# A Fourier layer with top-k experts on one core: first-stage groups placed in pairs, tables in twelve tiles, another expert gate and another key search

## The chip, the core and the metric

The kernel runs on one core of a Trainium2 chip. The metric is the device time of one execution in microseconds (us); lower is better. The engines that matter are TensorE (PE, with its weight loads shown apart as PEld), VectorE (DVE), ScalarE (ACT), GpSimd (POOL) and the queue of SyncE (SP), from which nearly all DMAs are issued.

## The reference, cut to what matters

Two layers follow each other on x of shape 8 x 3136 x 256. First a spectral layer: a real FFT over the 3136 positions, a complex 256 x 256 linear map with bias, a soft threshold on real and imaginary parts, and the inverse FFT. Then, in each of the 8 batches, a score per position, the 128 highest positions, an expert (256 -> 1024 -> 256, ReLU) on those rows only, weighted by a sigmoid of the score and added.

```python
X = np.fft.rfft(x, axis=1)                       # x: 8 x 3136 x 256
Yr = Xr @ w_r - Xi @ w_i + b_r
Yi = Xr @ w_i + Xi @ w_r + b_i
Yr = np.sign(Yr) * np.maximum(np.abs(Yr) - 0.01, 0.0)   # Yi likewise
y = np.fft.irfft(Y, n=3136, axis=1)
scores = y @ w_gate                              # 8 x 3136
for b in range(8):
    top = np.argpartition(-scores[b], 128)[:128]
    xe = y[b, top]
    ye = np.maximum(xe @ w1, 0) @ w2
    out[b, top] = xe + ye / (1 + np.exp(-scores[b, top]))[:, None]
```

## The kernel before

The FFT of length 3136 = 98 x 32 is done in two stages of small matmuls. **First stage** (`s1`): eight groups per batch; GpSimd or VectorE makes the sum and the difference of two halves of x (`xu`, `xv`, in `xsum_side`), TensorE multiplies them by a table (`quarters`: quadrants of 64 x 64 of the array, into two `s` banks of PSUM), ScalarE copies the banks out, and the result goes to scratch memory in HBM (`As`). **Second stage** (`s2`): per batch six units (`Q = 6`, so `T = 48` units in all); a unit loads 16 rows of `As` (tile `av`), does 64 small matmuls into the two `px` banks, and is split by ScalarE and VectorE into a high and a low part (`Xh`, `Xl`). **Spectral map** (`spectral`, full 128 x 128 array): 24 matmuls of 512 columns per unit into `py` banks, then bias and threshold (`shrink`). **Inverse** (`s2i`, 32 matmuls on strips of 32 rows into four `s` banks; then `s1i`, again eight groups per batch, with `cu`, `cv` and `cin` in the roles of `xu`, `xv` and `xt`) back to HBM through `Cs` and to the output. `s2i` also takes the score of each row of its banks (`score_part`).

**Selection** (`select`): the 128 highest scores of two batches together are found by a search over the bits of the threshold, three bits per round for the last two batches. A round counts by a bf16 comparison and a reduction on VectorE (`counts`), adds over the partitions by one small matmul (`ones`), and reads the counts (`digest`): which digits pass (`ok`), how many (`d`), the new prefix (`wp`, and a copy `w2`), and the keys of the next round (`f`), one after the other on VectorE. **Experts** (`gather`, `prepare`, `hidden`, `combine`): an indirect DMA fetches 128 rows, TensorE turns them, 32 plus 24 matmuls follow, and another indirect DMA scatters them into the output. The gate is a product and row sum on VectorE (`junk <- xe, wgb`) with a sigmoid on ScalarE. Experts use the two `py` banks.

The order of all instructions is fixed when the program is built: a planner keeps a clock per engine, and at every step picks among the candidates `middle` (spectral), `forward` (`s2`), `backward` (`s2i`), `forward1` (`s1`), `backward1` (`s1i`) and the threads of selection and experts the one with the least cost: the expected wait plus `STEP` times how far its place lies ahead of the current unit. The places of `s1` and `s1i` come from the lists `F1` and `I1` (units of a batch). Loads of constants wait for a number of stored and loaded pieces of batch 0 (`behind_a`, list `CA`). `warm` puts matmuls without use into gaps.

Of the kernel before, what the change touches and what calls it, by code (L numbers as in the profile page):

```python
# [22 lines left out]
P0 = 15  # L23
# [138 lines left out]
def fourier_moe(ctx: ExitStack, tc: tile.TileContext, x, w_r, w_i, b_r, b_i, wg, w1, w2,  # L162
# [184 lines left out]
    class Side:  # L347
        def __init__(self, g, low=None):
            self.g, self.over, self.need, self.low = g, False, None, low
            self.step()  # L350
# [14 lines left out]
    def side(g, low=None):  # L365
        s = Side(g, low)
        if not s.over:
            sides.append(s)
        return s
# [6 lines left out]
    def pump(t):  # L376
        again = True
        while again:
            again = False
            for s in list(sides):  # L380
                while not s.over:
                    w = s.when()
                    if w is None or w > t - (s.low() if s.low else 0.0):
                        break
                    s.step()
                    again = True
                    if s.low:
                        break
# [15 lines left out]

    first = c_tile([128, 2, 2, 64], F32, "first")
    sec = [c_tile([128, NJ, 64], F32, f"second{z}") for z in range(2)]
# [8 lines left out]
    wgb = c_tile([128, D], F32, "wgb")  # L415
    w1s = c_tile([128, 2, FF], F32, "w1s")
# [26 lines left out]
    def consts_s():  # L443
        yield "SP", behind_a(CA[0])
        ld(sec[0].rearrange("p j s -> p (j s)"), t_second[:, :NJ * 64])
        yield "SP", behind_a(CA[3])
        ld(tail, t_tail)
        yield "SP", behind_a(CA[4])
        ld(wgb, wg.rearrange("(o e) -> o e", o=1).broadcast_to([128, D]))
        ld(sec[1].rearrange("p j s -> p (j s)"), t_second[:, NJ * 64:])  # L450
# [16 lines left out]
    def consts_bias():  # L467
        vec.memset(m2l, -2.0 * LAM)
        yield "SP", behind_a(CA[2])
        for c, src in enumerate((b_r, b_i)):  # L470
            row = src.rearrange("(o e) -> o e", o=1)
            ld(bias[:, c, :], row.broadcast_to([128, D]))
            ld(bias_t[33 * c:33 + 31 * c], row.broadcast_to([33 - 2 * c, D]))
        yield "DVE", [bias, bias_t]
        vec.tensor_scalar(out=bias, in0=bias, scalar1=LAM, scalar2=None, op0=ALU.add)
        vec.tensor_scalar(out=bias_t, in0=bias_t, scalar1=LAM, scalar2=None, op0=ALU.add)
        made.add("bias")

    def consts_moe():
        yield "SP", lambda: pe["end"] if spec["t"] >= 1 else None  # L480
# [35 lines left out]
    def select(bs, bits, lag):  # L516
# [8 lines left out]
        low = lag  # L525

# [17 lines left out]
        def digest(tot, m, i, nxt):  # L544
# [31 lines left out]
            yield from counts(f, m2)  # L576

        rounds = [(2 ** (hi - i) - 1, i) for hi, i in zip([32] + cuts, cuts)]
        side(first_keys(rounds[0][0]), low)
        for (m, i), nxt in zip(rounds, rounds[1:] + [None]):  # L580
# [5 lines left out]
            hold(tot, name, side(digest(tot, m, i, nxt), low))  # L586
# [63 lines left out]
    def e_name():  # L650
        return "py" if spec["t"] >= T else m_name()

    def e_tile(shape):
        return new(ps, shape, F32, "py", 2) if spec["t"] >= T else m_tile(shape)

    def prepare(b, k, idx, xe, spare, st):
        n = min(128, cap - 128 * k)
        name = e_name()
        px = e_tile([128, 2, n])
# [4 lines left out]
        sg = new(pool, [n, 1], F32, "sg")  # L664
# [684 lines left out]
```

## Time and profile before

| what | us |
|---|---|
| median of 3 runs (700.66 to 705.55) | 703.77 |
| the profiled execution | 699.05 |
| its span, first to last instruction | 696.9 |
| TensorE busy | 672.4 (96%) |
| VectorE, ScalarE, GpSimd busy | 403.9, 360.1, 392.9 |
| DMA | 162.55 MB, mean 233 GB/s |

A busy time is a sum over instructions; matmuls overlap one another and their ends are modelled, so TensorE at 96% is not at its peak. The span falls into a start until the first spectral matmul, the spectral stage, and an end in which the last two batches are selected and all eight experts run.

### The profile page before, as it was taken

The numbers are of one execution on the slowest core, as the hardware profiler recorded it, in microseconds if no ns is written. First come the engines' busy times: TensorE is split into PE (matmuls) and PEld (weight loads), VectorE is DVE, ScalarE is ACT, GpSimd is POOL, SyncE is SP. The second block draws the span as 40 slices with busy tenths as digits, with TensorE's granted clock in tenths as the row PEclk, the third lists the DMA queues.
The fourth block names the chain that finished last, engine by engine and source line by source line (L and its number), as shares of the span: only waits on it lengthen the run. The fifth ranks groups of instructions, "written<-read, shape, count | busy, mean of one in ns | idle before, by whom it ended". The sixth has DMA issues, their size and how long they took to land.

```text
span 696.9 us, 19479 instructions
## 1 busy us (share of the span) xinstructions
PE 672.4 (96%) x7733; PEld 433.6 (62%) x7733; DVE 403.9 (58%) x1231; ACT 360.1 (52%) x766; POOL 392.9 (56%) x325
## 2 busy tenths in 40 slices
PE   8989999999999999999999999999999899989996
PEld 5546666566565656665566556666656566537896
DVE  7324454455356666774566676745776664478732
ACT  2335664655655656655566656565645445433111
POOL 4266654865866567767765767576434424453221
PEclk9989999999999999999999999999999999989999
DMA  8899878999799989998889889988794955584000
GB/s 237 283 288 304 264 241 260 252 302 270 224 234 302 285 292 200 319 276 287 197 326 274 311 212 327 273 265 187 257 265 131 213 156 161 175 246 147 31 31 24
DMA packets 85109, 162.55 MB, mean 233 GB/s; under 512 B 6333, under 2 KB 58906, under 8 KB 85018
## 3 DMA queue, kind: packets, MB, share of 16 engines
q1 hardware_dynamic: 83962, 159.13, 77.1%
q0 software_dynamic: 1056, 2.17, 1.0%
q8 instruction: 61, 1.00, 0.6%
q14 instruction: 30, 0.25, 0.1%
HBM read 83.23 MB, written 78.12 MB: 232 GB/s over the span
## 4 chain that ended last, share of the span: by engine, by line
PE 78%; DMA 7%; DVE 6%; issue 5%; ACT 1%; POOL 1%; SPq 0%; POOLq 0%; DVEq 0%; ACTq 0%
PE py L272 43%; PE s L272 26%; PE px L272 9%; DMA cin<-Ct 1%; DMA cin<-Cs 1%; DMA xe<-in_moe_w 1%; DVE px L220 1%; DVE r L220 1%; DMA As<-ot 1%; DMA xt<-in_x 1%; DVE c L220 1%; DMA av<-As 1%; DMA As<-at 1%; DVE junk L220 1%; POOL out L723 0%
## 5 line engine op out<-in xcount | busy, mean ns | idle before, releaser
L272 PE MATMUL py<-wh,Xh 128*128 128x512 f32 x384 | 168.0, 438 | 0.1
L272 PE MATMUL py<-wl,Xh 128*128 128x512 f32 x384 | 150.8, 393 | 0.1
L272 PE MATMUL py<-wh,Xl 128*128 128x512 f32 x384 | 150.3, 391 | 0.0
L272 PEld LDWEIGHTS py<-wh,Xh 128*128 128x128 f32 x384 | 72.1, 188 | 84.7 <-issue 62.7
L220 POOL TENSOR_TENSOR xu<-xt 113x512 f32<-113x512 f32 x56 | 72.0, 1286 | 90.5 <-PE s L272 76.1
L220 POOL TENSOR_TENSOR cu<-cin 113x512 f32<-113x512 f32 x56 | 72.2, 1289 | 82.4 <-PE s L272 72.3
L220 DVE TENSOR_TENSOR Xl<-px,Xh 128x512 fp32r<-128x512 f32 x96 | 61.9, 686 | 86.0 <-ACT Xh L220 85.9
L220 DVE CUSTOM_DVE_ANT_0 junk<-s,wgb 128x256 f32<-128x256 f32 x192 | 81.0, 422 | 51.3 <-ACT ct L220 37.8
L220 ACT COPY ot<-s 113x512 f32<-113x512 f32 x136 | 72.7, 596 | 62.6 <-PE s L272 56.2
L220 POOL TENSOR_TENSOR cv<-cin 113x512 f32<-113x512 f32 x64 | 85.7, 1341 | 11.3 <-DMA cin<-Cs 6.6
L220 ACT COPY at<-s 113x512 f32<-113x512 f32 x120 | 64.5, 593 | 52.9 <-PE s L272 45.2
L220 POOL TENSOR_TENSOR Y<-r,r 128x512 f32<-128x512 f32 x48 | 61.8, 1287 | 49.8 <-ACT r L220 36.4
L220 POOL TENSOR_TENSOR xv<-xt 113x512 f32<-113x512 f32 x60 | 78.2, 1304 | 8.7 <-DVE xt L220 4.9
L272 PEld LDWEIGHTS py<-wl,Xh 128*128 128x128 f32 x384 | 72.1, 188 | 17.1 <-issue 0.5
L272 PE MATMUL s<-cu,first 49*64 49x512 f32 (+1 forms) x256 | 76.5, 621 | 2.2 <-DVE ok L220 1.5
L272 PEld LDWEIGHTS py<-wh,Xl 128*128 128x128 f32 x384 | 72.6, 189 | 9.2
L220 ACT COPY ct<-s 128x256 f32<-128x256 f32 x192 | 57.8, 388 | 31.5 <-PE s L272 31.0
L272 PE MATMUL s<-xu,first 64*64 64x512 f32 (+1 forms) x256 | 71.4, 620 | 1.6 <-POOL xu L220 1.6
L272 PE MATMUL s<-cv,first 49*64 49x512 f32 (+1 forms) x256 | 71.8, 624 | 0.0
L272 PEld LDWEIGHTS px<-second,av 64*64 64x64 f32 x3072 | 52.6, 136 | 30.5 <-issue 15.0
L272 PE MATMUL s<-xv,first 64*64 64x512 f32 (+1 forms) x256 | 70.0, 623 | 0.0
L220 ACT CAST Xh<-px 128x512 fp32r<-128x512 f32 x96 | 51.7, 593 | 34.2 <-PE px L272 33.9
(135 smaller groups left out, 1002.8 us busy)
## 6 DMA issues: line engine op xcount, KB each, us to landing
out<-ot SPq DMA_DIRECT2D x64, 392.0 KB
av<-As SPq DMA_DIRECT2D x48, 512.0 KB
Cs<-ct SPq DMA_DIRECT2D x48, 512.0 KB
cin<-Cs SPq DMA_DIRECT2D x64, 384.0 KB
xt<-in_x SPq DMA_DIRECT2D x60, 392.0 KB
As<-at SPq DMA_DIRECT2D x60, 392.0 KB
cin<-in_x SPq DMA_DIRECT2D x4, 392.0 KB
As<-ot SPq DMA_DIRECT2D x4, 392.0 KB
```

Source lines behind the costliest of these rows:

```text
L220: return f(*args, **kw)
L272: return nc.tensor.matmul(out, a, b, start=start, stop=stop)
```

## The change

All places are laid anew: `F1` and `I1` put the eight groups of each batch 0.75 units apart, and the `s1` of one batch and the `s1i` of another get the same place (a pair, `NQ = 2`); batch 1, for which there is no inverse yet, has places of its own (`FB`), and the second unit waits for the first four spectral steps (`K0`). The tables of the second stage lie in twelve tiles (`fwd`, `bwd`), of which only the first is loaded at the start; weights, biases, the other tables, w1 and w2 are loaded later. Sums of batch 0 go to VectorE, those of the last batch to GpSimd; clearing of buffers goes to GpSimd but for one. The experts' gate is two matmuls with one column on TensorE, and the turned rows are copied out by ScalarE; experts may use `s` banks once the inverse second stage is done. For the last two batches the next round's keys are made from the prefix before last (`g`), ahead of `wp` and `w2`, and other sides step back for that search (`prio`). The units of the last two steps shrink on VectorE. Several weights of the planner change.

```diff
+                    if s.prio == 2 and s.need[0] == "DVE":
+                        u = [x for x in (x.when() for x in sides if x.prio == 0) if x is not None]
+                        if u and min(u) < w + UR:
+                            break
...
-    sec = [c_tile([128, NJ, 64], F32, f"second{z}") for z in range(2)]
+    fwd, bwd = [[c_tile([128, 4, 64], F32, f"{n}{g}") for g in range(Q)] for n in ("fwd", "bwd")]
...
-        yield "SP", behind_a(CA[0])
-        ld(sec[0].rearrange("p j s -> p (j s)"), t_second[:, :NJ * 64])
...
+        for n, t, src, w in sorted([(CS[0][g], fwd[g], t_second, 4 * g) for g in range(Q)] + [(CS[1][g], bwd[g], t_second, NJ + 4 * g) for g in range(Q)]
+                                   + [(CA[3], tail, t_tail, None), (CA[4], wgb, wg, None)], key=lambda x: x[0]):
+            yield "SP", behind_a(n)
...
-        yield "SP", lambda: pe["end"] if spec["t"] >= 2 else None
+        yield "SP", lambda: pe["end"] if spec["t"] >= CM else None
         ld(w1s, w1.rearrange("(h p) f -> p h f", p=128))
+        ld(wgc, wg.rearrange("(h p o) -> p h o", p=128, o=1))
...
-            yield "SP", lambda: pe["end"] if spec["t"] >= 3 + k // 2 else None
+            yield "SP", lambda: pe["end"] if spec["t"] >= CM + 1 + k // CN else None
...
+                if fast and nxt:
+
+                    m2 = nxt[0]
+                    f = f[:, :, :m2]
+                    vec.scalar_tensor_tensor(out=f, in0=d.broadcast_to([N1, nb, m2]), scalar=i, in1=st["g"],
+                                             op0=ALU.logical_shift_left, op1=ALU.bitwise_xor)
+                    yield "DVE", []
+                    yield from counts(f, m2)
                 for o in (wp, w2) if i else (wp,):
                     vec.scalar_tensor_tensor(out=o, in0=d, scalar=i, in1=st["w"], op0=ALU.logical_shift_left, op1=ALU.bitwise_xor)
+                if fast and nxt:
+                    st["w"] = w2
+                    ahead_keys(wp, after)
+                    return
...
+        def ahead_keys(wp, after):
+            if after:
+                m3, i3 = after
+                st["g"] = new(pool, [N1, nb, m3], U32, "g" + tag, 1)
+                vec.tensor_tensor(out=st["g"], in0=digits[:, 8 * i3:8 * i3 + m3].rearrange("p (o m) -> p o m", o=1).broadcast_to([N1, nb, m3]),
+                                  in1=wp.broadcast_to([N1, nb, m3]), op=ALU.bitwise_xor)
...
     def e_name():
-        return "py" if spec["t"] >= T else m_name()
+        if spec["t"] < T:
+            return m_name()
+        return "s" if ES and s2m["t"] >= T and open_at("s") < open_at("py") else "py"
...
-            yield "DVE", [px]
-            vec.tensor_copy(xT, px)
+            yield "ACT", [px]
+            act.copy(out=xT, in_=px)
             st["xT"] = True
-            yield "DVE", [xe]
-            junk = new(pool, [n, D], F32, "junk", 1)
-            vec.tensor_tensor_reduce(out=junk, in0=xe, in1=wgb[:n], scale=1.0, scalar=0.0,
-                                     op0=ALU.mult, op1=ALU.add, accum_out=sg)
...
+        for h in range(2):
+            mm(sg, xT[:, h, :], wgc[:, h, :], h == 0, h == 1)
...
-                    adder(t, b == 0).tensor_tensor(out=o, in0=t[:, 0, :], in1=t[:, 1, :], op=op)
+                    adder(t, 2 * (b == 0)).tensor_tensor(out=o, in0=t[:, 0, :], in1=t[:, 1, :], op=op)
...
-                    adder(t, last).tensor_tensor(out=o, in0=t[:, 0, :], in1=t[:, 1, :], op=op)
+                    adder(t, LA if last else 0).tensor_tensor(out=o, in0=t[:, 0, :], in1=t[:, 1, :], op=op)
...
-    EARLY, AHEAD, SW = 0.6,1.1,0.2
+    EARLY, AHEAD, SW = 0.6,1.5,0.2
...
-    STEP, THW, FIL = 5,4,(4,3)
+    STEP, THW, FIL = 3,4,(8,0.5)
...
-    F1, I1 = [-1, 0, 0, 1, 2, 2, 3, 3],[10, 10, 11, 12, 12, 13, 14, 15]
+    F1, I1 = [-1.75, -1.0, -0.25, 0.5, 1.25, 2.0, 2.75, 3.5],[10.25, 11.0, 11.75, 12.5, 13.25, 14.0, 14.75, 15.5]
...
-    NQ = 1
-    CA = 1,2,8,9,10,9
+    NQ = 2
+    CA = 1, 8, 8, 12, 11, 0, 12
+    CS, CM = ((0, 8, 9, 10, 11, 12), (11, 12, 13, 14, 14, 14)),42
+    FB = .25, .5, .75, 1.25, 1.5, 2, 2.5, 3
+    CN, K0 = 4,4
+    WS = 1.0
+    CX = 10, 10, 10, 10, 11, 11, 11, 12
...
+    TE, LV, UR, FS, ES, LA, HP = 0,2,0.5,True,True,3,False
...
-        if n >= T or quad(n) not in av or n > spec["t"] + 1 or len(X) > 1:
+        if n >= T or quad(n) not in av or n > spec["t"] + 1 or len(X) > 1 or n == 1 and spec["k"] < K0:
...
-            vec.memset(t[:P0].rearrange("p a c -> p (a c)") if len(t.shape) == 3 else t[:P0].rearrange("p a c d -> p (a c d)"), 0.0)
+            (gps if z else vec).memset(t[:P0].rearrange("p a c -> p (a c)") if len(t.shape) == 3 else t[:P0].rearrange("p a c d -> p (a c d)"), 0.0)
...
-            if spec["t"] >= T or at == 0:
+            if spec["t"] >= T or at == 0 and (0, 7) in summed:
                 warm(c[1])
```

## Rows read from the trace of the kernel before

**Rows 1.** Windows: us, busy us per engine, clock, DMA share, GB/s

```profile
0.00:24.00 24.00, 20.68 (x103) 10.75 (x104) 16.96 (x19) 9.87 (x18) 13.26 (x12) 1.00 0.86 272
24.00:30.70 6.70, 6.70 (x31) 5.49 (x30) 0.30 (x1) 1.92 (x4) 0.00 (x0) 1.00 0.70 239
...
38.70:45.50 6.80, 6.79 (x29) 2.54 (x32) 0.00 (x0) 1.07 (x2) 5.34 (x5) 0.50 1.00 302
46.50:590.00 543.50, 534.99 (x6731) 338.09 (x6727) 324.96 (x1031) 314.93 (x674) 336.26 (x279) 1.00 0.87 255
590.00:635.00 45.00, 42.31 (x281) 21.62 (x280) 27.86 (x78) 19.91 (x42) 24.13 (x17) 0.89 0.69 199
635.00:692.00 57.00, 54.16 (x437) 50.23 (x429) 31.33 (x100) 10.48 (x26) 10.13 (x11) 1.00 0.12 40
```

**Rows 2.** Timeline of the start: start us, us, engine line op out<-in xcount

```profile
35.18 1.16 PE L272 MATMUL px<-second,av 64*64 64x64 f32 x64 [0.74 <-DMA av<-As]
...
37.00 1.29 DVE L220 TENSOR_TENSOR Xl<-px,Xh 128x512 fp32r<-128x512 f32 x2 [3.48 <-ACT Xh L220]
...
46.46 0.50 PE L272 MATMUL py<-wh,Xh 128*128 128x512 f32 x1
```

**Rows 3.** Chain that ended last, in order of time: start us, us, what

```profile
24.89 5.76 DMA As<-ot
...
43.59 1.92 PE s L272 x8
...
50.16 1.02 PE s L272 x8
...
571.02 1.58 PE py L272 x6
...
574.47 2.26 PE py L272 x9
...
582.63 1.73 PE s L272 x32
...
644.17 3.03 PE py L272 x24
```

**Rows 4.** Groups by line: busy us, mean ns of one, idle before

```profile
L220 ACT COPY ot<-s 113x512 f32<-113x512 f32 x136 | 72.7, 596 | 62.6 <-PE s L272 56.2 <-DMA out<-ot 4.1 <-PE px L272 1.2
...
L220 POOL TENSOR_TENSOR cu<-cin 113x512 f32<-113x512 f32 x56 | 72.2, 1289 | 82.4 <-PE s L272 72.3 <-DMA av<-As 5.2 <-DMA cin<-Ct 4.6
...
L220 DVE TENSOR_TENSOR cu<-cin 113x512 f32<-113x512 f32 x8 | 8.1, 1017 | 6.1 <-DMA cin<-Cs 3.4 <-PE s L272 1.6 <-DMA cin<-Ct 1.1
...
L220 DVE CUSTOM_DVE_ANT_0 junk<-xe,wgb 128x256 f32<-128x256 f32 x8 | 4.5, 558 | 0.0
...
L220 DVE SCALAR_TENSOR_TENSOR hl<-py,hh 128x512 fp32r<-128x512 f32 x10 | 6.9, 689 | 7.3 <-ACT hh L220 7.3
```

**Rows 5.** Timeline of VectorE in the last search

```profile
606.67 0.17 DVE L220 TENSOR_SCALAR px<-px 98x2 int32<-98x2 f32 x1 [3.42 <-PE px L272]
...
641.66 0.16 DVE L220 TENSOR_SCALAR ok<-px 98x14 f32<-98x14 f32 x1
...
642.06 0.17 DVE L220 SCALAR_TENSOR_TENSOR px<-px,w 98x2 uint32<-98x2 uint32 x1
642.26 0.16 DVE L220 SCALAR_TENSOR_TENSOR w<-px,w 98x2 uint32<-98x2 uint32 x1
...
644.53 0.16 DVE L220 TENSOR_SCALAR ok<-px 98x14 f32<-98x14 f32 x1
...
654.20 0.16 DVE L220 TENSOR_SCALAR px<-px 98x2 uint32<-98x2 f32 x1
...
663.25 0.16 DVE L220 TENSOR_TENSOR idxs<-col,px 128x2 uint32<-128x2 f32 x1
```

**Rows 6.** Timeline of TensorE in the expert after the search

```profile
664.38 3.74 PE L272 MATMUL py<-xT,w1s 128*128 128x128 f32 x32
```

**Rows 7.** Timeline of GpSimd: the last scatter

```profile
692.89 0.97 POOL L723 DMA_INDIRECT out<-ye,idxs  x1 [6.48 <-DVE ye L220]
```

More of the change, by code (lines that the diff above doesn't have):

```diff
@@ L347, in fourier_moe, with __init__ @@
     class Side:
-        def __init__(self, g, low=None):
-            self.g, self.over, self.need, self.low = g, False, None, low
+        def __init__(self, g, low=None, prio=1):
+            self.g, self.over, self.need, self.low, self.prio = g, False, None, low, prio
             self.step()
@@ L468, in consts_bias @@
         vec.memset(m2l, -2.0 * LAM)
[L469 to L477, printed above, removed]
+        for z, (t, n) in enumerate(((bias, 128), (bias_t, 33))):
+            yield "SP", behind_a(CA[2 + 4 * z])
+            for c, src in enumerate((b_r, b_i)):
+                row = src.rearrange("(o e) -> o e", o=1)
+                if z:
+                    ld(t[33 * c:33 + 31 * c], row.broadcast_to([33 - 2 * c, D]))
+                else:
+                    ld(t[:, c, :], row.broadcast_to([n, D]))
+            yield "DVE", [t]
+            vec.tensor_scalar(out=t, in0=t, scalar1=LAM, scalar2=None, op0=ALU.add)
+            made.add("bias" if z == 0 else "bias_t")
     def consts_moe():
-        yield "SP", lambda: pe["end"] if spec["t"] >= 1 else None
+        yield "SP", lambda: pe["end"] if spec["t"] >= 3 else None
         ld(wq, t_wq)
@@ L525, in select @@
         low = lag
+        last = bs.stop == B
+        fast = last and FS
         def counts(f, m):
@@ L576, in digest @@
             yield from counts(f, m2)
+            if fast:
+                ahead_keys(wp, after)
+        def ahead_keys(wp, after):
[4 more added lines that the diff above has]
+                                  in1=wp.broadcast_to([N1, nb, m3]), op=ALU.bitwise_xor)
         rounds = [(2 ** (hi - i) - 1, i) for hi, i in zip([32] + cuts, cuts)]
-        side(first_keys(rounds[0][0]), low)
-        for (m, i), nxt in zip(rounds, rounds[1:] + [None]):
+        side(first_keys(rounds[0][0]), low, 0 if last else 1)
+        for (m, i), nxt, after in zip(rounds, rounds[1:] + [None], rounds[2:] + [None, None]):
             yield lambda: avail([st["n"]]) if st["n"] is not None else None
@@ L585, in select @@
             st["n"] = None
-            hold(tot, name, side(digest(tot, m, i, nxt), low))
+            hold(tot, name, side(digest(tot, m, i, nxt, after), low, 0 if last else 1))
         yield lambda: avail([st["n"]]) if st["n"] is not None else None
@@ L685, in hidden @@
             name = e_name()
-            ph = e_tile([128, 4, n])
+            ph = e_tile([128, 4, n], name)
             for f in range(4):
+                if f and SP:
+                    yield [xT]
                 for h in range(2):
@@ L695, in halves @@
                 act.activation(out=hs[q][0], in_=ph, func=AF.Relu)
+                if HP and spec["t"] >= T and len(settled) < B and b < B - 2:
+                    full = new(pool, [128, 4, n], F32, "r1")
+                    hold(full, "r1", both_side[0])
+                    act.activation(out=full, in_=ph, func=AF.Relu)
+                    yield "POOL", [full, hs[q][0]]
+                    gps.tensor_tensor(out=hs[q][1], in0=full, in1=hs[q][0].bitcast(F32), op=ALU.subtract)
+                    st["h", q] = True
+                    return
                 yield "DVE", [ph, hs[q][0]]
@@ L702, in hidden, with combine @@
             else:
-                yield lambda: avail([t for h in hs for t in h]) if all(st["h", z] for z in range(FF // 512)) else None
-    def combine(b, k, idx, xe, ga, hs, st):
+                yield lambda: avail(list(hs[0])) if st["h", 0] else None
+    def combine(b, k, idx, xe, xT, ga, hs, st):
         n = min(128, cap - 128 * k)
-        drain(st["gate"])
         name = e_name()
-        py = e_tile([n, D])
+        pe_y = e_tile([n, D + 1], name)
+        py, sg = pe_y[:, :D], pe_y[:, D:]
+        for h in range(2):
+            mm(sg, xT[:, h, :], wgc[:, h, :], h == 0, h == 1)
         for f in range(FF // 128):
+            if f == 4:
+                yield lambda: avail(list(hs[1])) if st["h", 1] else None
+            elif f and SP:
+                yield []
             hh, hl = [t[:, f % 4, :] for t in hs[f // 4]]
@@ L713, in put @@
         def put():
+            yield "ACT", [sg]
+            act.activation(out=ga, in_=sg, func=AF.Sigmoid)
             yield "DVE", [py, ga]
@@ L1156, in middle @@
         if k == 8:
-            if YT:
+            if YT or "bias_t" not in made:
                 return None
@@ L1190, in run @@
             s2m["t"] += 1
-            if g == Q - 1:
-                s2m["tail"] = True
-        return n + LAG, max(avail([Y[b, g]]), open_at("s", 4)), run, "q"
+            if g == tg(b):
+                s2m["tail"] = b
+        return n + LAG, max(avail([Y[b, g], bwd[g]]), open_at("s", 4)), run, "q"
     def forward1():
@@ L1290, in fourier_moe @@
                     cost = THW * wait + c[0]
+                elif spec["t"] >= T and TB is not None and c[4] is backward:
+                    cost = THW * wait + TB
+                elif spec["t"] >= T and T1 is not None and c[4] is backward1:
+                    cost = wait + T1
                 else:
```

100 lines of the change are left out of this document (55 added, 45 removed).

## The prediction

> **What bounds the kernel now.** I read the windows first [rows 1], since one share of busy time for the whole span hides that it has three parts. A start lasts until the first spectral matmul at 46.5 us. The spectral stage, 46.5 to 590, has TensorE busy for 535.0 of 543.5 us while the DMA engines are busy for 0.87 of it at 255 GB/s: it is TensorE's. The end lasts 106.9 us, to 696.9; in its first 45 us the granted clock averages 0.89 and the DMA share is 0.69, and after 635 TensorE is at 54.2 of 57 us and DMA at 0.12. Then I read each part where its last wait ends: the start in the chain and the timeline of the first second-stage unit [rows 2, 3], the stage in the lengths of TensorE's pieces in the chain [rows 3], the end in VectorE's search and the last scatter [rows 5 to 7].
>
> In the start the reader should see that everything hangs on the last store of `As`, issued at 24.89 and landed at 30.65 [rows 3]; only then may `av` be loaded, and its first matmul is at 35.18 [rows 2]. X is split by 38.29 [rows 2], yet the first spectral matmul comes at 46.46: 8.2 us go to three groups of the next batch, to the second unit's `px`, and to waits between them, at a granted clock of 0.50, the lower level of 1.2 GHz [rows 1].
>
> **The start, part by part.** Is the store late because of work or of bytes? By 30.7 us DMA has moved 272 GB/s x 24 + 239 x 6.7 = 8.13 MB [rows 1]. What the program has issued by then is 8 loads of x and 8 stores of `As` of 0.401 MB each (6.42), the first table 0.13, the whole forward table 0.79, weights 0.52 and biases 0.33: 8.19 MB. So it is bytes. After, 6.42 + 0.13 + one table tile of 0.13 = 6.68 MB stand ahead of the last store; the old curve has 6.53 MB at 24.0, so the store lands near 24.6. VectorE's sums of batch 0 (16 instead of 8) and GpSimd's clearing are off this path as long as they feed a group per 1.5 us or so; a `cu` sum that runs beside one of GpSimd costs 1.02 us on VectorE [rows 4], so two of them would give 2.0 us per group, 16 us for eight, and a last store still issued before 24. From the landing to `px` it was 35.18 - 30.65 = 4.5 us [rows 2, 3]. Now weights, biases and the second tile (0.92 MB) are issued in the same moment on the same SP queue: between 0 and 0.92 MB / 255 GB/s = 3.6 us later [rows 1]; I take half, 1.8. X takes 38.29 - 35.18 = 3.1. First spectral matmul: 24.6 + 4.5 + 1.8 + 3.1 = 34.0 instead of 46.5, -12.5. What stood before it comes behind it: three groups at 1.02 and one `px`, near 1.1 too, 4.1 us [rows 3]. **Net -8.4**, bounds -13 (store earlier, nothing ahead of `av`) and -3 (weights or biases last, or groups at the lower level).
>
> The other tables move later within batch 0, and w1, w2 and their splits from the first units to units 42 to 45. They are the same bytes and instructions, 2 MB of them for w1 and w2, into a stage whose DMA engines have 0.13 of their time free [rows 1]; I cost them at nothing. Without that cover they cost 2 MB / 255 GB/s = 8 us once. Behind each of them on SP stand loads of `av` and stores; on ScalarE the casts of w2 stand ahead of X, as they did before.
>
> **The stage.** A piece of 9 spectral matmuls takes 2.26 us, one of 6 takes 1.58 [rows 3]: 0.227 us each and 0.22 us per piece for going to the quadrant shapes and back. There are 124 such excursions in the stage, from 50.16 to 582.63 [rows 3]. With the new places I count per batch 8 pairs, 6 places where `px` and `s2i` meet, less 2 that coincide with a pair, and one for the tail: 13, or 104. 20 x 0.22 = **-4.4 us**. Bounds: nothing (`px` and `s2i` stay apart) and, if the even spacing also removes the waits that TensorE still has, -4.4 - 8.5 = -13 (543.5 - 535.0, [rows 1]). That pairs ask for more banks at once is a rival below.
>
> **The end.** Two chains meet here. *The search*: 47.5 us from its first step to its last (606.67 to 654.20), though an undisturbed round is 644.53 - 641.66 = 2.87 [rows 5]; eleven such would be 31.6. The rest is disturbance: eight `cu` sums at 1.02, gate products at 0.56, slowed rounds while TensorE lacks work. The change takes two steps of 0.20 (`wp`, `w`) off ten rounds, giving 2.47, and all sums and gate products off VectorE; the 12 `hl` of the first six experts, 0.69 each, remain [rows 4, 5]. 10 x 2.47 + 2 + half of the `hl`, 4.1 = 31; with PE's queue in between I take 34, -13.5. The last batch's 16 sums then fall to GpSimd, 16 x 1.29 = 20.6 us [rows 4], done long before the indices. From the search's end to the indices stay 9.1 us, from the indices to the last scatter it was 29.6 [rows 5, 7], which is where four experts were still queued. *TensorE*: an expert is 3.6 (32 matmuls, [rows 6]) + 3.0 (24, [rows 3]) + 0.3 turned = 6.9 us, eight are 55; 13 groups at 1.02, two `s2i`, selection and scores make 19; the new gates have no row, and lie between nothing and 4 instructions at the 0.117 of the hidden matmuls [rows 6], 3.7 in all; I take the upper end, since they load weights of the same size: 78 us. Packed without a gap the end is 78 + 4 (scatter issue to the end of the span, [rows 7]) = 82; unpacked as now it is 107. Experts on four more banks may start their next half without waiting, and after 635 TensorE is already at 95% [rows 1], so the loss to recover lies before that. By the other chain the indices come near 590 + 60 (16.7 until the search's first step, 34, 9.1), and gather, two experts, waits and scatter give some 26 more: 86. I take 90: **-17**, bounds -25 and 0.
>
> **Sum**: -8.4 - 4.4 - 17 = -29.8. The profiled execution's 699.05 becomes 669.3; the median of the runs shown is 703.77 / 699.05 = 1.0068 of it, so 673.8.
>
> **Rivals.** *DMA takes back the start.* From 38.7 to 45.5 the DMA engines are full at 302 GB/s [rows 1], and an earlier first unit needs the same `av`, x and stores sooner. Against it: over the stage the share is 0.87. Then the start gives nothing: 699.05 - 21.4, 682 on the runs' scale. 0.15. *The first groups run at the lower level.* Useless matmuls filled TensorE until the first group; now they come only when all of batch 0 is summed. At 0.50 a group took 1.92 instead of 1.02 [rows 3]; eight times 0.9 is 7.2 us if it delays the last store, 681. Against it: bytes, not groups, set that store, and the clock was granted in full from 0 to 24 [rows 1]. 0.08. The Trainium skill (TensorE: Matmul & The Clock Gate, Part 1: The HAM clock gate) says that the throttled level is the default and activity releases it, which speaks for this rival; the rows show the lower level only after a gap. *The end is not shortened*: search steps and experts wait for each other in the queues as now, and only 12.8 is gained, 691. 0.13. *Nothing in sum*: planned order and real order drift apart and waits eat it, 697 to 711. 0.10. *Slower*: a pair fills all four `s` banks, and four evictions of 0.596 [rows 4] are 2.4 us; `s2i` needs four free banks, and behind a pair with only a `px` of 1.1 between it waits 1.3 us. 29.8 / 1.3: from 23 of the 48 units on the gain is gone; in all 48 it costs 62, 736 by the runs' scale. For it: `s2i` is placed beside two of eight pairs. Against it: the planner counts open banks. 0.08, near 720.
>
> **How the numbers follow.** The forecast, all three gains at about their size, has 0.46, and its own range is 652 (-13, -13 and -25, or 648.1 by the profiled execution) to 690. Faster by over 1% (a measurement of this kernel tells about that much from no change) is 0.46 + 0.15 + 0.08 + 0.13 = 0.82; within it 0.10; slower 0.08. The range 650 to 701 takes in the three smaller gains and some 2 us for the spread of runs at the low end, and leaves out about 0.18.
>
> **What would show it.** Right: the first spectral matmul near 34; some 104 excursions; the last stage of the search with rounds near 2.5 and no `cu` or `junk <- xe` on VectorE; from the last spectral matmul to the end about 90 us, with the last two experts alone behind the indices. Wrong: `av` landing later than 33 with DMA full; `s2i` waiting for ScalarE's `at` and `ot` in unit after unit; a search still near 47 us; or a stage longer than 545 us.

## The result, and the profile after

The changed kernel takes 676.75 us (median of 4 runs, 676.50 to 677.83); the kernel before took 702.21 beside it (4 runs). The ratio is 0.9638, 95% interval 0.9590 to 0.9685: faster. The profiled execution took 676.51 us with a span of 674.7; before it was 699.05 and 696.9. The forecast was 673.8.

Units are counted from 0 to 47 here, six to a batch. A unit begins with its first spectral matmul, and "the seventh unit" of the expectations is unit 6. The span of either kernel, cut at these points:

| stretch | before, us | after, us | difference | forecast |
|---|---|---|---|---|
| until the first spectral matmul | 46.46 | 38.16 | -8.3 | -12.5 |
| units 0 to 5 | 56.93 | 64.28 | +7.35 | +4.1 (moved work) |
| units 6 to 46 | 477.59 | 466.89 | -10.7 | -4.4 |
| unit 47 and the end | 115.92 | 105.37 | -10.55 | -17 |
| sum | 696.9 | 674.7 | -22.2 | -29.8 |

Windows of the kernel after: stretch, its length, busy us of PE, PEld, DVE, ACT and POOL with instructions, granted clock, DMA share, GB/s. The third is units 0 to 5, and the end begins at 583 (compare [rows 1]).

```profile
0.00:24.00 24.00, 18.15 (x93) 9.02 (x94) 11.27 (x18) 9.78 (x17) 6.41 (x9) 1.00 0.82 268
24.00:38.20 14.20, 12.64 (x117) 10.67 (x116) 3.87 (x7) 3.40 (x6) 0.39 (x1) 1.00 0.94 253
38.20:102.40 64.20, 62.69 (x861) 39.95 (x859) 27.25 (x67) 35.21 (x72) 42.44 (x41) 1.00 0.87 262
102.40:583.00 480.60, 474.51 (x5989) 297.96 (x5981) 300.29 (x968) 279.91 (x609) 300.16 (x244) 1.00 0.89 258
583.00:635.00 52.00, 49.70 (x407) 34.22 (x405) 34.55 (x125) 23.91 (x49) 33.10 (x28) 1.00 0.69 200
635.00:674.70 39.70, 31.77 (x265) 30.14 (x263) 11.39 (x30) 7.11 (x20) 7.04 (x8) 0.98 0.08 28
```

The start, from the timelines of TensorE and then of SP: start us, us, engine, line, operation, out<-in, with the idle time before it in brackets. [Rows 2, 3] are the lines of before that answer to these.

```profile
5.85 1.11 PE L272 MATMUL s<-xu,first 64*64 64x512 f32 x1 [5.85 <-DVE xu L220]
...
9.06 1.05 PE L272 MATMUL s<-xv,first 64*64 64x512 f32 x1
...
15.57 3.29 PE L272 MATMUL py<-first 128*128 128x256 f32 x14
...
20.13 0.59 PE L272 MATMUL s<-xu,first 64*64 64x512 f32 x1
...
20.67 11.06 PE L272 MATMUL py<-first 128*128 128x256 f32 x50
33.28 1.16 PE L272 MATMUL px<-fwd,av 64*64 64x64 f32 x64 [1.55 <-DMA av<-As]
34.38 3.95 PE L272 MATMUL s<-wh 128*128 128x512 f32 x16
38.16 0.39 PE L272 MATMUL py<-wh,Xh 128*128 128x512 f32 x1
```

```profile
22.07 0.31 SPq L301 DMA_DIRECT2D As<-ot  x1
...
27.05 0.93 SPq L301 DMA_DIRECT2D av<-As  x2
```

The last store of `As` is issued at 22.07, and `av` could be loaded at 27.05. The `py <- first` and `s <- wh` rows are `warm`'s matmuls without use. One run of them stands ahead of the last two first-stage groups, one behind the last group, one between `px` and the first spectral matmul; X was ready at 36.4 (`Xl` starts at 35.09 and takes 1.29), but TensorE was still in the third.

The end (compare [rows 5, 7]). The timeline of VectorE: the search's first step, its first three and its last `ok`, its last step, and the indices. Then that of GpSimd: the gather of an expert, and the last three of the five scatters behind the indices.

```profile
596.74 0.17 DVE L220 TENSOR_SCALAR px<-px 98x2 int32<-98x2 f32 x1 [1.51 <-PE px L272]
...
600.79 0.17 DVE L220 TENSOR_SCALAR ok<-px 98x14 f32<-98x14 f32 x1
...
603.78 0.17 DVE L220 TENSOR_SCALAR ok<-px 98x14 f32<-98x14 f32 x1 [0.74 <-PE px L272]
...
606.55 0.16 DVE L220 TENSOR_SCALAR ok<-px 98x14 f32<-98x14 f32 x1
...
632.57 0.16 DVE L220 TENSOR_SCALAR ok<-px 98x14 f32<-98x14 f32 x1
...
634.14 0.17 DVE L220 TENSOR_SCALAR px<-px 98x2 uint32<-98x2 f32 x1 [0.22 <-PE px L272]
...
642.40 0.16 DVE L220 TENSOR_TENSOR idxs<-col,px 128x2 uint32<-128x2 f32 x1
```

```profile
644.15 0.96 POOL L676 DMA_INDIRECT xe<-out,idxs  x1 [8.95 <-DVE ye L220]
...
655.02 0.98 POOL L772 DMA_INDIRECT out<-ye,idxs  x1 [2.09 <-DVE ye L220]
662.87 0.97 POOL L772 DMA_INDIRECT out<-ye,idxs  x1 [6.87 <-DVE ye L220]
670.71 0.97 POOL L772 DMA_INDIRECT out<-ye,idxs  x1 [6.88 <-DVE ye L220]
```

From its first step to its last the search takes 37.4 us (596.74 to 634.14) instead of 47.5. Its nine rounds from the first `ok` to the last take 31.8 us, 3.53 each; the shortest takes 2.77 (606.55 - 603.78) and not 2.47. The last scatters are 7.85 us apart: one expert behind the other.

### The profile page after: what moved, and what is told of

Its sections match the earlier page's. It is cut to its first block, busy times and chain, and to the rows that moved or that the text cites. A ratio compares the mean times of both kernels' runs of the same rounds, so it can differ in the third digit from the quotient of the medians.

```text
span 674.7 us, 19503 instructions
## 1 busy us (share of the span) xinstructions
PE 649.5 (96%) x7716; PEld 422.0 (63%) x7716; DVE 388.6 (58%) x1214; ACT 359.3 (53%) x772; POOL 389.5 (58%) x328
## 4 chain that ended last, share of the span: by engine, by line
PE 80%; DMA 8%; issue 5%; DVE 3%; POOL 2%; ACT 1%; POOLq 0%; SPq 0%; DVEq 0%; ACTq 0%
PE py L272 45%; PE s L272 26%; PE px L272 9%; DMA As<-at 2%; DMA xt<-in_x 2%; DMA av<-As 1%; DMA cin<-Cs 1%; DMA As<-ot 1%; DVE r L220 1%; POOL out L772 1%; DVE c L220 1%; DVE px L220 1%; DMA xe<-in_moe_w 1%; ACT r L220 0%; POOL xe L676 0%
## 5 line engine op out<-in xcount | busy, mean ns | idle before, releaser
L220 POOL TENSOR_TENSOR cu<-cin 113x512 f32<-113x512 f32 x64 | 82.2, 1284 | 51.0 <-PE s L272 44.7
L220 ACT COPY ot<-s 113x512 f32<-113x512 f32 x136 | 73.4, 596 | 34.9 <-PE s L272 27.6
L220 POOL TENSOR_TENSOR cv<-cin 113x512 f32<-113x512 f32 x64 | 82.1, 1283 | 0.0
L220 POOL TENSOR_TENSOR Y<-r,r 128x512 f32<-128x512 f32 x46 | 59.3, 1289 | 23.7 <-ACT r L220 11.5
L272 PE MATMUL s<-cu,first 64*64 64x512 f32 (+1 forms) x256 | 72.5, 604 | 0.3 <-DVE Csc L220 0.3
L220 POOL TENSOR_TENSOR xv<-xt 113x512 f32<-113x512 f32 x56 | 72.1, 1287 | 0.0
L272 PE MATMUL s<-cv,first 64*64 64x512 f32 (+1 forms) x256 | 70.7, 606 | 0.2 <-POOL cv L220 0.2
L272 PEld LDWEIGHTS px<-fwd,av 64*64 64x64 f32 x3072 | 51.0, 135 | 26.2 <-issue 10.4
L220 ACT ACTIVATE r<-r,m2l 128x512 f32<-128x512 f32 x46 | 33.4, 726 | 61.7 <-DVE r L220 38.7
```

Of the source, the lines that this page charges most:

```text
L220: return f(*args, **kw)
L272: return nc.tensor.matmul(out, a, b, start=start, stop=stop)
```

## The experiments

All are the changed kernel with one thing altered. The table gives the median of the timed runs, the ratio to the kernel before, timed beside it, and marks of the profiled execution.

| run | us | ratio, 95% interval | span | unit 0 | unit 6 | unit 47 | indices |
|---|---|---|---|---|---|---|---|
| before | 702.21 | 1 | 696.9 | 46.5 | 103.4 | 581.0 | 663.3 |
| after | 676.75 | 0.964, 0.959 to 0.969 | 674.7 | 38.2 | 102.4 | 569.3 | 642.4 |
| fill_late | 680.02 | 0.973, 0.967 to 0.979 | 675.7 | 35.1 | 105.1 | 571.6 | 644.9 |
| fb_late | 672.00 | 0.964, 0.956 to 0.972 | 671.8 | 34.1 | 100.8 | 567.2 | 641.2 |
| tables_first | 678.75 | 0.977, 0.968 to 0.985 | 676.4 | 42.5 | 105.2 | 570.5 | 644.3 |
| w_early | 682.68 | 0.979, 0.968 to 0.991 | 682.4 | 38.2 | 104.7 | 573.0 | 648.2 |
| places_old | 715.54 | 1.024, 1.018 to 1.030 | 712.1 | 37.8 | 103.2 | 609.6 | 685.4 |
| planner_old | 712.13 | 1.023, 1.015 to 1.030 | 710.7 | 40.5 | 105.1 | 590.0 | 657.4 |
| plan_old | 711.79 | 1.015, 1.009 to 1.020 | 706.7 | 42.8 | 103.6 | 589.0 | 653.6 |
| keys_old | 678.71 | 0.969, 0.964 to 0.975 | 677.4 | 40.2 | 102.7 | 569.9 | 650.4 |
| py_only | 681.86 | 0.976, 0.970 to 0.982 | 677.5 | 38.4 | 104.2 | 569.7 | 643.7 |
| sums_dve | 683.58 | 0.976, 0.970 to 0.982 | 677.9 | 37.8 | 102.2 | 569.5 | 651.6 |
| bufs | 677.16 | 0.965, 0.960 to 0.971 | 672.3 | 40.1 | 102.7 | 569.6 | 641.4 |
| late_bufs | 675.03 | 0.962, 0.956 to 0.967 | 674.0 | 36.8 | 102.3 | 569.4 | 643.2 |

How finely can this be read? after, keys_old, py_only, sums_dve and bufs have the same start, and still their unit 0 begins at 37.8 to 40.2 and their unit 6 at 102.2 to 104.2. From there units 6 to 46 are the same within 2 us in all runs with the new plan other than w_early (465.3 to 467.3). So marks within 2 us of each other are not told apart, and of the timed runs only gaps that their intervals don't bridge.

### The start

**fill_late**: matmuls without use only once the eight stores of `As` are issued, and without the microsecond by which they may outlast a wait.

```diff
-            if spec["t"] >= T or at == 0 and (0, 7) in summed:
+            if spec["t"] >= T or at == 0 and stored.get(("A", 0), 0) == 8:
-    WS = 1.0
+    WS = 0.0
```

> The kernel after, with two lines of its filler changed: fillers (matmuls without use) at the start come only once all eight first-stage groups of batch 0 are issued, and they are planned 1 us shorter. Theory 1 (fillers overshoot: in the trace of after, fillers run from 15.57 to 18.8 us while the sums of group 7 are ready at 16.5, and from 34.4 to 38.1 while X is split at 36.4): the last store of As is issued near 19 instead of 22.1, the first spectral matmul comes near 34 instead of 38.2, and the time falls by 3 to 4 us, to about 673. Rival (the start hangs on bytes or on the clock): the store lands no earlier or the granted clock falls to 0.50 around the first unit; the first spectral matmul stays within 1 us of 38.2 and the time within 1 us of 676.8.

The last store is issued at 18.92, `av` at 24.76, and unit 0 begins at 35.12: the prediction had the store land near 24.6 and unit 0 at 34.0. But unit 1 lasts 20.1 us instead of 11.7, unit 6 begins no earlier, and the time is 680.02, not the 673 of the first theory. Windows of fill_late, then its ScalarE and TensorE timelines:

```profile
35.10:56.00 20.90, 20.90 (x289) 12.68 (x287) 6.51 (x10) 8.06 (x15) 17.75 (x15) 1.00 0.98 262
56.00:66.00 10.00, 5.80 (x44) 2.17 (x40) 1.99 (x4) 4.69 (x9) 4.96 (x4) 0.77 0.98 318
```

```profile
53.14 1.07 ACT L220 COPY at<-s 113x512 f32<-113x512 f32 x2 [4.82 <-DMA As<-at]
59.46 1.07 ACT L220 COPY at<-s 113x512 f32<-113x512 f32 x2 [5.25 <-DMA As<-at]
...
60.19 0.61 PE L272 MATMUL s<-xu,first 64*64 64x512 f32 x1 [3.84 <-ACT at L220]
```

The DMA engines are full (share 0.98). ScalarE cannot copy a first-stage group of batch 1 out, because the buffer's earlier store has not landed; TensorE waits for the bank for 3.84 us; from 56 to 66 us the granted clock is 0.77, so part of that stretch runs at the lower level of 1.2 GHz. That is the first rival, a transfer that takes the start back. The changed kernel has a weaker form of it (lines of ScalarE, VectorE and TensorE):

```profile
58.49 1.07 ACT L220 COPY at<-s 113x512 f32<-113x512 f32 x2 [4.78 <-DMA As<-at]
...
60.18 0.69 DVE L220 SCALAR_TENSOR_TENSOR Y<-py,r 128x512 f32<-128x512 f32 x1 [2.77 <-ACT r L220]
...
60.93 0.50 PE L272 MATMUL py<-wh,Xh 128*128 128x512 f32 x1 [1.51 <-DVE Y L220]
```

ScalarE waits 4.78 us for an earlier store of `at`, its next step `r` and VectorE's `Y` come late by it, and TensorE waits 1.51 us.

**fb_late**: fill_late, with batch 1's loads released later and its groups later.

```diff
-    FB = .25, .5, .75, 1.25, 1.5, 2, 2.5, 3
+    FB = 1, 1.5, 1.75, 2.25, 2.5, 3, 3.25, 3.5
-    CX = 10, 10, 10, 10, 11, 11, 11, 12
+    CX = 10, 11, 12, 12, 13, 13, 14, 14
```

> fill_late (no fillers in the start once the stores are issued) with the loads of the second batch's x released one to three steps later and its first-stage groups placed half a unit to a unit later. If what stopped fill_late at 60 us was the second batch's traffic going ahead of the first batch's (DMA engines full, TensorE waiting 3.8 us for a buffer whose store had not landed), that wait shrinks below 1 us, the seventh unit begins near 98 to 100, and the run gains 2 to 4 us on the changed kernel. If the sum of bytes until the seventh unit sets it, the wait only moves: the seventh unit begins at 102 to 106 and the run is 0 to 4 us above the changed kernel.

Unit 0 begins at 34.14, unit 1 is back to 12.3 us, and the wait for `at` is 1.46, in unit 3, which lasts 15.8 instead of 9.5. Unit 6 begins at 100.8; with the same start in late_bufs it is 102.3. At most 1.6 us of the 4.0 are left there, and by the spread above even that is not shown.

**tables_first**: all six forward tiles at the start.

```diff
-    CS, CM = ((0, 8, 9, 10, 11, 12), (11, 12, 13, 14, 14, 14)),42
+    CS, CM = ((0, 0, 0, 0, 0, 0), (11, 12, 13, 14, 14, 14)),42
```

> The changed kernel, with all six forward table tiles loaded at the start instead of one at the start and five behind the stores: 5 x 0.131 = 0.655 MB more ahead of the last store of As, the same bytes in sum. By the prediction's step (bytes ahead of the store set the start, and the start sets the rest) the store and the first spectral matmul come 0.655 MB / 0.255 MB per us = 2.6 us later, 38.2 becomes 40.7, and so does the run, about +2.6 us. By the rival that DMA takes the start back (its engines are full until 80 us, so only the sum of bytes counts) the first spectral matmul is late by the same 2.6 but the seventh unit begins at 102.4 as in the changed kernel, within 1 us, and the run changes by less than 1 us.

`av` is issued at 29.23 instead of 27.05 (+2.2, near the +2.6 of the bytes), unit 0 begins 4.35 later, unit 6 2.75 later, unit 47 1.2 later. That lies between the two theories, and the last mark is within the spread.

**w_early**: w1 and w2 in units 2 to 6 as before.

```diff
-    CS, CM = ((0, 8, 9, 10, 11, 12), (11, 12, 13, 14, 14, 14)),42
+    CS, CM = ((0, 8, 9, 10, 11, 12), (11, 12, 13, 14, 14, 14)),2
-    CN, K0 = 4,4
+    CN, K0 = 2,4
```

> The changed kernel, with w1 and w2 loaded (2.1 MB) and w2 split in units 2 to 6 as before the change, instead of units 42 to 45. If they are free in both places, as the prediction costed them, the run stays within 1.5 us. If the DMA engines set the first 80 us, 2.1 MB at 0.29 MB per us are 7 us: the seventh unit begins between 105 and 109 instead of 102.4, and the run is 3 to 7 us longer, less what units 42 to 47 gain (at most 2).

Unit 6 begins 2.3 us later, unit 12 4.3 (171.4 against 167.1), unit 47 3.7; units 42 to 46 gain 0.5. So 2.1 MB are not free in the early place, at about half of the 7 us that their bytes take; this rests on the marks of unit 12 and unit 47, since the timed intervals overlap. The rest of its longer span is in the end, where a part of TensorE's work happened to run at the lower level (granted clock in its first 10 us; 1.00 in the changed kernel from 583 on):

```profile
585.80:595.80 10.00, 8.86 (x61) 6.21 (x59) 4.45 (x20) 3.13 (x9) 0.22 (x1) 0.66 0.40 127
```

### The stage

**places_old**: the uneven places of before, no pairs.

```diff
-    F1, I1 = [-1.75, -1.0, -0.25, 0.5, 1.25, 2.0, 2.75, 3.5],[10.25, 11.0, 11.75, ...]
+    F1, I1 = [-1, 0, 0, 1, 2, 2, 3, 3],[10, 10, 11, 12, 12, 13, 14, 15]
-    NQ = 2
+    NQ = 1
```

> The kernel after with the places of first-stage groups of before (F1, I1 and NQ = 1), all else as after. Theory 1 (the prediction's step: pairs save changes between full array and quadrants): some 20 more excursions than after's 136 and a stage about 4.4 us longer, 681. Theory 2 (from the trace: after has 136 excursions against 124 of before, so pairs saved none): excursions fall to about 125, and the time stays within 2 us of 676.8. Theory 3 (even spacing takes waits away): the stage grows by over 6 us by waits of TensorE, not by excursions.

**planner_old**: the planner's weights and look-aheads of before.

```diff
-    EARLY, AHEAD, SW = 0.6,1.5,0.2
-    BACK, TAIL = 99,46
-    LAST = 0
-    PF = (0,0.1)
-    BEGIN, RATE, DB = 2.5,2.2,0.1
-    AHEADT, FA, TD = 0.7,0,0
-    DG, GAP = 9,0.5
-    STEP, THW, FIL = 3,4,(8,0.5)
+    EARLY, AHEAD, SW = 0.6,1.1,0.2
+    BACK, TAIL = 99,40
+    LAST = 3
+    PF = (0,0.3)
+    BEGIN, RATE, DB = 2.5,2.2,0.5
+    AHEADT, FA, TD = 1.3,2,0
+    DG, GAP = 0.5,0.5
+    STEP, THW, FIL = 5,4,(4,3)
```

> The changed kernel with the planner's weights and look-aheads of before (about a dozen constants), and the new places, pairs, tables, keys, gate and banks. The prediction gave these constants no price. If the even places alone make the stage, the run stays within 3 us of the changed kernel and the stage near 545. If places and constants only work together, the stage becomes 555 or longer and the run 10 us or more longer, and the 35 us of places_old are a mismatch rather than the worth of the places.

**plan_old**: the two diffs above together.

> The changed kernel with both the places of before (uneven, no pairs) and the planner's constants of before; tables, keys, gate, banks and the later w1 and w2 stay new. places_old and planner_old had each made units 6 to 42 longer (438 and 426 us against 415.6; the kernel before has 422.2). If places and constants are one choice, units 6 to 42 come back near 422, units 42 to 47 near 55, and the run is 8 to 14 us above the changed kernel. If each half of the new plan is worth its own loss, the losses add: units 6 to 42 at 445 or more and the run above 730.

Units 6 to 41 as windows, of before, after, plan_old, planner_old and places_old in this order:

```profile
103.40:525.60 422.20, 417.36 (x5235) 258.37 (x5228) 255.59 (x828) 250.86 (x537) 276.74 (x223) 1.00 0.90 265
```

```profile
102.40:518.00 415.60, 409.93 (x5185) 255.50 (x5178) 253.07 (x818) 242.95 (x523) 265.60 (x213) 1.00 0.90 265
```

```profile
103.60:526.60 423.00, 416.76 (x5235) 257.74 (x5228) 255.51 (x828) 249.39 (x532) 273.49 (x219) 1.00 0.89 264
```

```profile
105.05:531.30 426.25, 420.25 (x5220) 259.79 (x5212) 253.42 (x828) 247.29 (x528) 267.92 (x215) 1.00 0.87 259
```

```profile
103.20:541.50 438.30, 425.11 (x5211) 259.60 (x5204) 256.44 (x826) 247.91 (x528) 271.03 (x218) 0.99 0.87 255
```

With the whole old plan the stretch is 423.0, before it was 422.2: tables, keys, gate and banks do nothing here, and the plan is worth 7.4 us. Of these some 3 us are work that now stands outside the stretch: two groups (360 and 344 matmuls of `s1` and `s1i` instead of 368 and 352) and one `s2i` (1120 matmuls instead of 1152). Half a plan is worse here than either: +10.7 with the old constants, +22.7 with the old places. For the latter TensorE's waits in the stretch say where 8.6 us of that go; they are for steps of the selections that now meet it at another time (us in total, times, longest):

```profile
PE px L272 <- DVE n L220: 5.2, 2, 2.6
PE py L272 <- DVE r L220: 2.7, 1, 2.7
PE px L272 <- DVE mask L220: 2.3, 1, 2.3
```

In the changed kernel the first of them is 1.6 and the others are gone; `s2i` takes another 9.1 (below). Of the theories of places_old the third came nearest.

Outside the stretch plan_old met neither of its two forecasts. Units 42 to 46 take 62.4 us in it (58.7 in planner_old, 68.1 in places_old), where the kernel before has 55.4 and the changed one 51.3, and the time is 35.0 us above the changed kernel, not 8 to 14, and even above the kernel before (ratio 1.015, 1.009 to 1.020). planner_old is 35.4 us slower and places_old 38.8. So going back to one half costs about as much as going back to both: with the old constants the places make no difference that the intervals show, with the new ones they make 39 us. That is what a mismatch costs, not what even places are worth alone. Without the new plan the rest of the change gains nothing; the reverse, the new plan without the rest, was not run.

The number of excursions to the quadrant shapes, counted over the timeline, is the same: 100 in units 6 to 41 before, 100 after (over the stage 124 and 130, not 104). Counted as gaps between two spectral matmuls in which such work stands, it is 99 and 92, over the stage 121 and 119: at 0.22 us each that is 1.5 us at most. What became shorter is `s2i`. Against 1.05 us for its 32 matmuls, its pieces in units 6 to 41 took 6.5 us too long in sum before, 0.6 after, 2.2 in plan_old, 0.5 in planner_old and 9.7 in places_old.

### The end

**keys_old**: the next keys again from the new prefix (`wp`, `w2` first).

```diff
-    TE, LV, UR, FS, ES, LA, HP = 0,2,0.5,True,True,3,False
+    TE, LV, UR, FS, ES, LA, HP = 0,2,0.5,False,True,3,False
```

> The kernel after with the key search of before for the last two batches (next keys behind the prefix; FS off). Theory 1 (the prediction: the search sets the end): two more VectorE steps of 0.20 us on ten rounds, the search 4 us longer and the time 4 us longer, 681. Theory 2 (TensorE's queue of experts sets the end: in the trace of after five of eight scatters come behind the indices): the search takes 2 to 4 us more, but the time stays within 1.5 us of 676.8.

**sums_dve**: the last batch's sums shared between VectorE and GpSimd again.

```diff
-    TE, LV, UR, FS, ES, LA, HP = 0,2,0.5,True,True,3,False
+    TE, LV, UR, FS, ES, LA, HP = 0,2,0.5,True,True,1,False
```

> The changed kernel, with the last batch's sixteen cu and cv sums shared between VectorE and GpSimd as before the change instead of all on GpSimd. By the prediction's step (sums of 1.02 us disturb the search, and the search sets the end): some eight sums come back, the search lasts 37.4 + up to 8 us, and the run grows by 4 to 8 us. If the search is no longer what sets the end (as keys_old suggests, where it ended 8 us later and the run grew by 2.7), the run grows by 0 to 2 us.

**py_only**: experts on the two `py` banks alone.

```diff
-    TE, LV, UR, FS, ES, LA, HP = 0,2,0.5,True,True,3,False
+    TE, LV, UR, FS, ES, LA, HP = 0,2,0.5,True,False,3,False
```

> The kernel after with experts on the two py banks alone (ES off). Theory 1 (more banks let experts run ahead; most of the end's gain): the end grows from 91.7 us by 6 to 10, time 683 to 687. Theory 2 (experts wait for their row buffers and scatters, not for banks): within 2 us of 676.8.

I measure the end from the last matmul of the tail's map: 92.0 us in the changed kernel (582.7 to 674.7), 91.0 to 92.4 in fill_late, tables_first and fb_late, whose end is the same. Returning the keys makes it 94.2, the sums 94.5, the banks 94.0. The search reacts more: from the first to the last `ok` it takes 31.8 us after, 33.9 with the old keys, 40.7 with the sums on VectorE. The indices come 8.0 (keys_old) and 9.2 us (sums_dve) later than in the changed kernel, yet the span grows by 2.7 and 3.2:

```profile
651.64 0.16 DVE L220 TENSOR_TENSOR idxs<-col,px 128x2 uint32<-128x2 f32 x1
...
673.85 0.97 POOL L772 DMA_INDIRECT out<-ye,idxs  x1 [6.85 <-DVE ye L220]
```

These are sums_dve's indices and last scatter. Behind its indices 26.2 us remain, in the changed kernel 32.3: while the search is slow, TensorE works off experts that otherwise stand behind it. By these spans about a third of a later index is paid. The timed runs leave more open: the profiled executions of sums_dve and py_only are the fastest of their four, and the medians lie 6.8 and 5.1 us above the changed kernel's, with intervals just above its own. For the sums that is inside the 4 to 8 us that the prediction's step gives. For keys_old, 2.0 us above, the intervals overlap. The banks lengthen the end by 2.0 us, not by the 6 to 10 of the first theory.

What the planner's constants do to the end is larger. It is 107.0 us before, 109.3 in plan_old, 111.2 in planner_old, but 91.4 in places_old, which has the old places and the new constants. Windows until the last `ok` and behind it, of before, after and plan_old:

```profile
589.90:652.20 62.30, 58.86 (x407) 36.23 (x406) 42.09 (x122) 23.35 (x49) 26.40 (x19) 0.92 0.56 163
652.20:696.90 44.70, 37.80 (x308) 35.63 (x306) 17.59 (x56) 7.14 (x18) 8.82 (x9) 0.97 0.08 28
```

```profile
582.70:632.60 49.90, 47.60 (x388) 32.11 (x387) 32.71 (x115) 23.83 (x49) 31.61 (x27) 1.00 0.72 206
632.60:674.70 42.10, 34.17 (x285) 32.54 (x284) 13.23 (x42) 7.18 (x21) 8.81 (x9) 0.98 0.09 29
```

```profile
597.40:644.60 47.20, 44.71 (x291) 22.48 (x290) 28.83 (x106) 19.60 (x46) 27.39 (x22) 1.00 0.69 203
644.60:706.70 62.10, 56.30 (x478) 54.54 (x476) 19.02 (x51) 12.91 (x29) 12.76 (x13) 1.00 0.09 29
```

plan_old's search is the shortest of the three, and its end the longest, since TensorE fills the search with matmuls without use instead of experts. TensorE's groups by line from 597.4 to 644.6 (busy us, mean ns):

```profile
L272 PE MATMUL py<-wh 128*128 128x512 f32 x53 | 14.9, 410 | 0.0
L272 PE MATMUL py<-xT,w1s 128*128 128x128 f32 x32 | 4.1, 281 | 0.0
```

That is the first half of one expert, and 53 matmuls without use; of the second halves of the eight experts (192 matmuls) 5 are done by the last `ok`. In the changed kernel 73 are, three experts, and no matmul without use stands there. The kernel before has 72 done by then, beside 25 matmuls without use; it takes 62.3 us for that, at a granted clock of 0.92, and the changed kernel 49.9 at 1.00.

**bufs**: a fourth row buffer, and the expert's output in the ring of three.

```diff
-        xe = new(pool, [n, D], F32, "xe", 3)
+        xe = new(pool, [n, D], F32, "xe", 4)
...
-            ye = new(pool, [n, D], F32, "ye", 1)
+            ye = new(pool, [128, 4, D], F32, "ct", 3)[:n, 0, :]
```

> The changed kernel with a fourth row buffer for the experts (gathers may run four ahead at the end) and the expert's output row block in the free ring of three buffers of the spectral output instead of one buffer. If what stands between the indices (642.40) and the end (674.7) is buffers, that is the gather that waits for a row buffer (644.15 and 651.95 instead of directly behind the indices) and the output that waits for the scatter before it (5 to 6 us at 649.90), the last three scatters move together and the run is 3 to 5 us shorter. If the last experts are serial for their own chain (32 matmuls, halves, 24 matmuls, turn), the run stays within 1 us.

The gathers stand directly behind the indices, and no output waits for a scatter any more:

```profile
641.78 0.98 POOL L676 DMA_INDIRECT xe<-out,idxs  x1 [8.91 <-DVE idxs L220]
643.10 0.96 POOL L676 DMA_INDIRECT xe<-out,idxs  x1 [0.34 <-DVE ct L220]
...
652.37 0.97 POOL L772 DMA_INDIRECT out<-ct,idxs  x1 [5.70 <-DVE ct L220]
660.22 0.97 POOL L772 DMA_INDIRECT out<-ct,idxs  x1 [6.88 <-DVE ct L220]
668.22 0.97 POOL L772 DMA_INDIRECT out<-ct,idxs  x1 [7.03 <-DVE ct L220]
```

Behind the indices 30.9 us remain instead of 32.3, and the last three scatters are still 7.85 and 8.00 apart. The waits were there, but an expert's own chain hid most of them.

**late_bufs**: fb_late and bufs together.

> fb_late and bufs together: no fillers in the start once the stores are issued, the second batch's loads and groups later, and more buffers at the end. If the start and the end are separate accounts, the gains add: fb_late's 2.9 us of span (671.8 against 674.7) and whatever bufs gives, near 668 to 670 on its own if the buffers matter. If the end's search and expert chain only re-pack, it stays at fb_late's 671 to 673.

675.03 us over 6 runs (671.47 to 680.90); the gains don't add. Neither this nor fb_late or bufs is shown to beat the changed kernel: their ratios to before, 0.962, 0.964 and 0.965, lie in its interval.

## Why the prediction was near, and where it was wrong

The time came out 2.95 us above the forecast, and part of that is luck. The spans shrank by 22.2 us and not by 29.8: the start gave 7.4 us less than forecast, the stage 6.3 more, the end 6.4 less. On the scale of the profiled executions 669.3 was forecast and 676.51 came; the median is nearer because the kernel before was profiled 4.7 us below its median and the changed kernel at its median.

**Start: -1.0 instead of -8.4.** The step from bytes to the last store was right but not alone: without the fillers ahead of the last two groups the store lands where it was put (`av` issued at 24.76 in fill_late). As the change was made, fillers delayed the last stores by 2.3 us (27.05 against 24.76) and stood 1.8 us behind X (36.4 to 38.16; in fill_late 1.9, 33.2 to 35.12). The step that failed comes later: the share of 0.87 over the whole stage was taken to leave the first units free time too, in "I cost them at nothing" and in the small chance for the DMA rival. Whether unit 0 begins at 34.1 or at 46.5 us, unit 6 begins between 100.8 and 105.2, the kernel before included. The DMA engines are at 0.93 in the kernel before and at 0.86 to 0.98 in the runs looked at from 24 to 72 us, and there an earlier start meets buffers whose stores have not landed (fill_late), while later traffic moves the wait (fb_late) and 2.1 MB more cost about 4 us (w_early). So the first rival came true for this part. That full transfers are all of it is not shown: of the 7.35 us by which units 0 to 5 grew, 4.0 are three groups and one `px` more, 1.5 the wait behind `Y`, and the rest `s2i` and spectral pieces that took longer.

The three groups were not all the start's, as the prediction counted. TensorE's timeline of the kernel before has two between X and unit 0 (37.96 and 43.52), and matmuls without use for 2.5 us between them; the third came from units 6 to 41.

**First groups at the lower level.** The first three groups did run slowly: a matmul took 1.05 to 1.11 us until about 10 us, 0.59 at 20.13, with nothing on TensorE before 5.85. The granted clock stands at 1.00 for this window and doesn't show it. The Trainium skill (TensorE: Matmul & The Clock Gate, Part 1: The HAM clock gate) has the throttled level as the default; the durations agree. What it cost is not separated: the last store depended on the fillers further on, and fill_late, with the same slow groups, has the store where the bytes put it.

**Stage: -10.7 instead of -4.4.** The step that failed is the count of excursions, 130 and not 104; at most 1.5 us come from there. About 2 us are two groups that went into the stretches ahead and behind. The upper bound named the real place, waits, but they stand inside `s2i` and in the last units: `s2i` lost 5.9 us of excess in units 6 to 41, while TensorE's idle time there went from 4.8 to 5.7 us, and units 42 to 46 took 51.3 us instead of 55.4, with TensorE idle for 0.2 instead of 3.4. places_old, planner_old and plan_old show that places and constants make this together; the prediction gave the constants no price at all. The rival of a bank jam behind pairs did not occur: `s2i` waits less than before.

**End: -10.55 from unit 47, -15.0 from the last matmul of the tail's map (before 107.0, after 92.0), instead of -17.** Some 4.5 us went into unit 47 instead (8.9 us to this matmul before, 13.4 after), which now has one more `s2i` and a group of `s1i`. The search took 37.4 us where 34 was forecast, since its rounds are still disturbed: in the shortest an `Xl` of 0.68 us stands ahead of the `ok`, in others the `ok` waits for TensorE's count (0.74 us in the second `ok` shown). But it begins 14.0 us behind that matmul and not 16.8, and the indices come after 59.7 us, where 60 was forecast and 73.4 stood before. The sums are worth 9 us of search and the keys 2, as forecast in kind. The step that failed is what stands behind the indices: 32.3 us and not 26 (33.7 before). Five of the eight scatters are there, not those of two experts, and TensorE's own queue decides: an expert takes 7.85 us. In the sum it had 6.9 and 0.46 for its gate; the 0.49 on top are about its wait for `xT` (0.52), and eight times that makes the packed 82 into 86. The other 6 us to 92.0 are not assigned.

In span, keys, sums and banks are worth 2 to 3 us each; by the timed runs sums and banks may be worth more, and the gate was not tried alone. What lets an earlier index count at all is that TensorE gets the same three experts done beside a shorter search, without fillers, and that needs the new constants: with the old ones the same functions end later than before, with either set of places. Which of the constants does it was not tried; that the price of an expert's step at the end falls from 3 to 0.5 (`FIL`) is the likely one, but only argued.

## What to carry to other kernels

When the start of a pipeline is shortened, follow the bytes past the first matmul: read the gain behind the stretch in which the transfers are full, here at unit 6. A hand-made order and the constants that tune it are one edit; here going back to either half cost 35 to 39 us, as much as going back to both, so test them together before giving the difference to one. A search that is sped up shortens the end only as far as the engine that has the rest of the work gets that work done beside it; measure what that engine does meanwhile, matmuls without use counted as idle, and not the search alone.

## What the runs showed of the hardware

- A wait can cost more than its length. Around a wait of 3.84 us (fill_late) TensorE's granted clock was 0.77 over 10 us; in fb_late, behind a wait of 1.46 us, nine spectral matmuls took 3.55 us instead of 2.28. Not every such wait does: around the 1.51 us of the changed kernel (60.93) the clock stayed at 1.00.
- The granted clock of a window can read 1.00 while matmuls take 1.05 us that take 0.59 later: durations of one kind show the level at the beginning of an execution, the column doesn't.
- The same start, in five programs, put the first spectral matmul anywhere from 37.8 to 40.2 us, with DMA engines nearly full; units 6 to 46 then repeated within 2 us.
